# A gated recurrence with a soft mixture of experts on one core: TensorE fillers until a later plan time, the logarithm pinned ahead of the first tanh, new instruction lists

## The chip, the cores and the metric

The kernel runs on one core of one Trainium2 chip. The metric is the time of one execution on the device in microseconds (us); lower is better. The core has five instruction streams: PE (TensorE, matrix products and transposes), DVE (VectorE), ACT (ScalarE), POOL (GpSimd), and SP, which here only starts transfers (DMA). Each stream runs its instructions in the order in which the program lists them and waits on semaphores for the others.

## The reference

There are 4 sequences of 5056 tokens with 256 channels, so 20224 rows. A gated linear recurrence runs along each sequence, and its result goes through a soft mixture of 8 experts with 4 slots each (32 slots).

```python
# recurrence
sig_r, sig_i = sigmoid(r_gate), sigmoid(i_gate)
a_t  = exp(8 * sig_r * log(clip(sigmoid(a_param))))
norm = sqrt(max(1 - a_t * a_t, 1e-6))
h    = a_t[:, t] * h + (norm * sig_i * x)[:, t]        # over t, y[:, t] = h
# soft mixture of experts on x = y
logits = x @ phi
d = exp(logits - max over tokens) / sum over tokens
slot_out[e] = relu((d.T @ x)[e] @ w1[e]) @ w2[e]
c = exp(logits - max over slots) / sum over slots
out = c @ slot_out
```

The softmax over all tokens means that no output row can be made before the whole recurrence is done. The kernel has therefore a first part (the recurrence and running sums, to about 210 us), a short middle (the expert products, to about 232 us) and an output part.

## The kernel before, in words

Tokens are cut into 40 quads of 512 tokens (the last is shorter), and these into 21 units: quad 0 alone, then pairs, then quad 39 alone. In names, a number after a unit's letters is the unit (for U, YC and TY the quad), and .0 or .1 is the half of the channels. For one unit the steps are:

- Dr, Di, Dx (SP): loads of r_gate, i_gate and x, up to 1 MiB each.
- SR, SI (ACT, `mk_sr`, `mk_si`): tanh of the two gates. EX (ACT): a_t by exp, over two units at a time. RT (ACT): the square root. Exp and tanh share one table of ACT's functions, the square root needs another, and so does the logarithm, so ACT loads a table at each change. SA and LN (ACT, `e_sa`, `e_ln`) make the vector `ca` from a_param once: exp and then Ln, after which the table with exp and tanh is loaded. CA (DVE) clips it.
- SQ (POOL, DVE or ACT): a_t squared, a product of two SBUF tiles. U (POOL or DVE): the input gate times x, also two SBUF tiles. The string `IV` says for each quad how: D is one DVE instruction ((i+1)*x), E is i*x by one product, after which PE adds x while it transposes, P is an extra POOL step P1 (i+1) and then the product.
- TU (PE): transposes of the product into PSUM. ST (DVE): times the norm. SC (DVE): the recurrence as a scan, which needs the scan of the unit before. LG, TY (PE), YC (DVE or ACT), LE, AE (DVE), ES, DM (ACT), LD, PD (POOL): logits, y with tokens in partitions, running maxima, exponentials and sums over groups of four quads.

The middle is MT to SL (merging the sums), L1 and L2 (PE, the experts, with weights w1 and w2 loaded by SP), SO, RS and SW. The output part has, for each group, CT (PE), CM, CS (DVE), CE (ACT), RR, RB, RC, CN (POOL), TB (PE) and HE: the softmax over slots, transposed back. Then for each unit come OT (PE, 8 products into four banks of PSUM), OE (DVE or ACT, a copy of one bank) and OD (SP, the store).

Which engine does what in which order is written out: `ORDER` holds a list for each engine, and a list B for the order in which SBUF slots and POOL's and DVE's turns are claimed. The class `Planner` replays these lists with a duration for every step (its `alt` gives that on the other engine). The replay decides two more things: which buffer each step gets, and where PE gets a filler. A filler (`WU`, line 1220) is two transposes of the identity into a free bank. It is put wherever the replay finds PE with nothing to do before the plan time `WARMT`, and it stands in PE's list from then on. The replay ends when its last real step ends.

Of the kernel before, what the change touches and what calls it, by code (L numbers as in the profile page):

```python
# [26 lines left out]
IV = 'DDDEEEEEEEEEEEEEEDEEEEEEEDDPEPEPEPPPPPPD'  # L27
# [16 lines left out]
WARMT = 245.0  # L44
# [57 lines left out]
    ),  # L102
    "ACT": (
# [11 lines left out]
    ),  # L115
# [38 lines left out]
    ),  # L154
}
SWITCH = 0.09
# [1459 lines left out]
```

## Time and profile before

| | |
|---|---|
| runs | 290.07, 290.78, 291.12 us; median 290.78 |
| the profiled execution | 290.38 us, its span 288.4 us |
| busy share of the span | PE 86%, DVE 82%, ACT 83%, POOL 61% |
| transferred | 100.04 MB, HBM read 78.94 MB, written 20.71 MB |
| granted TensorE clock, mean | 0.943 of full speed |

The span runs from the first to the last instruction that the profiler shows; the execution's own time is 2.0 us longer. In the rows below a time is counted from the start of the span, "x8" is a count of instructions, and "<-" in square brackets names what ended the idle time ahead of an instruction. PEclk is the granted clock: 1.00 is 2.4 GHz and 0.50 is 1.2 GHz.

### The profile page before, as it was taken

Reading aid. Unit: us, or ns where it says so; the run is one execution under the profiler, and the core shown is the slowest. Engines: PE = TensorE matmul, PEld = TensorE weight load, DVE = VectorE, ACT = ScalarE, POOL = GpSimd, SP = SyncE. Lnnn points to the kernel's source line nnn. Section 1 sums busy time; section 2 is a strip of 40 time slices with the busy share of each in tenths; the row PEclk is TensorE's granted clock in tenths of the full one; section 3 lists DMA queues with packets and bytes.
Section 4 is the critical chain, followed back from the end, with each engine's and each line's share of the span. In section 5 each row is a group of like instructions: output and inputs, shape, how many; then the busy total and the mean of one; then the engine's idle time right before and its main releaser. Section 6 shows DMA issues by size and latency. Waiting matters only on the chain.

```text
span 288.4 us, 6115 instructions
## 1 busy us (share of the span) xinstructions
PE 247.2 (86%) x2523; PEld 190.0 (66%) x2523; DVE 235.9 (82%) x268; ACT 238.3 (83%) x231; POOL 175.2 (61%) x138
## 2 busy tenths in 40 slices
PE   8999798779887877988799989999899999968750
PEld 8999797549665645757468767666565576745540
DVE  0217999999999999999999999999979376885630
ACT  6999899999999989999999999999932267754450
POOL 4022969988999699996989989994030620031000
PEclk9999999979999999999999999999999999975755
DMA  7999999999994998959999999998930049999987
GB/s 279 431 420 424 417 418 418 423 419 423 410 408 157 384 405 331 401 169 353 370 350 400 330 427 414 379 393 352 347 136 2 5 164 414 416 415 409 399 335 330
DMA packets 14987, 100.04 MB, mean 347 GB/s; under 512 B 1904, under 2 KB 2160, under 8 KB 3184
## 3 DMA queue, kind: packets, MB, share of 16 engines
q1 hardware_dynamic: 14816, 99.65, 85.9%
q8 instruction: 20, 0.33, 0.4%
q14 instruction: 7, 0.06, 0.1%
q10 hardware_dynamic: 144, 0.00, 0.0%
HBM read 78.94 MB, written 20.71 MB: 346 GB/s over the span
## 4 chain that ended last, share of the span: by engine, by line
DVE 50%; PE 25%; ACT 10%; issue 10%; DMA 1%; POOL 0%; ACTq 0%; POOLq 0%; SPq 0%; DVEq 0%
DVE all_s L935 21%; DVE pair L915 13%; PE bank L1516 7%; DVE yn L974 5%; DVE all_s L848 3%; PE bank L1334 3%; PE one L1516 2%; ACT all_s L792 2%; PE bank L1380 2%; ACT all_s L863 2%; PE pair L892 2%; DVE all_s L1034 2%; PE bank L1490 2%; DVE all_s L827 2%; ACT yn L972 1%
## 5 line engine op out<-in xcount | busy, mean ns | idle before, releaser
L935 DVE TENSOR_TENSOR_SCAN all_s<-all_s,pair 128x1024 f32<-128x1024 f32 (+8 forms) x48 | 92.8, 1950 | 0.6
L829 POOL TENSOR_TENSOR all_s<-all_s 128x1024 f32<-128x1024 f32 x33 | 79.0, 2413 | 5.2 <-ACT all_s L807 4.8
L848 POOL TENSOR_TENSOR all_s<-all_s 128x1024 f32<-128x1024 f32 (+1 forms) x33 | 62.4, 1908 | 28.5 <-ACT all_s L863 26.1
L892 PE MATMUL pair<-ident,all_s 128*128 128x128 f32 x488 | 60.9, 276 | 8.8 <-DVE all_s L935 6.8
L892 PEld LDWEIGHTS pair<-ident,all_s 128*128 128x128 f32 x488 | 53.1, 140 | 18.2 <-DVE all_s L935 7.8
L958 PE MATMUL pair<-ident,all_s 128*128 128x128 f32 x316 | 41.8, 277 | 8.2 <-DVE all_s L935 6.2
L958 PEld LDWEIGHTS pair<-ident,all_s 128*128 128x128 f32 x316 | 34.4, 140 | 17.9 <-DVE all_s L935 9.9
L915 DVE SCALAR_TENSOR_TENSOR pair<-all_s,pair 128x1024 f32<-128x1024 f32 (+1 forms) x38 | 44.6, 1184 | 0.0
L1220 PE MATMUL one<-ident 128*128 128x128 f32 x342 | 41.6, 282 | 1.4 <-POOL ident masks.py:199 1.4
L863 ACT ACTIVATE all_s<-all_s,ca 128x2048 f32<-128x2048 f32 (+3 forms) x24 | 42.3, 1791 | 0.0
L1467 POOL TENSOR_TENSOR all_s<-all_s,rs_all 128x512 f32<-128x512 f32 (+3 forms) x12 | 10.5, 895 | 50.8 <-DVE rs_all L1464 50.8
L1220 PEld LDWEIGHTS one<-ident 128*128 128x128 f32 x342 | 39.8, 146 | 2.0 <-POOL ident masks.py:199 1.4
L875 ACT ACTIVATE all_s<-all_s 128x2048 f32<-128x2048 f32 (+2 forms) x21 | 37.2, 1807 | 2.3 <-DVE all_s L848 1.4
L807 ACT ACTIVATE all_s<-all_s 128x2048 f32<-128x2048 f32 (+2 forms) x21 | 37.8, 1806 | 0.0
L792 ACT ACTIVATE all_s<-all_s 128x2048 f32<-128x2048 f32 (+2 forms) x21 | 37.5, 1804 | 0.0
L1018 PE MATMUL one<-all_s,phi_sb 128*32 128x256 f32 (+1 forms) x328 | 24.8, 402 | 3.3 <-DVE all_s L1447 1.4
L1531 ACT COPY all_s<-bank 128x512 f32<-128x512 f32 (+1 forms) x34 | 18.8, 584 | 9.2 <-PE bank L1516 5.6
L1533 DVE COPY all_s<-bank 128x512 f32<-128x512 f32 (+1 forms) x29 | 18.5, 655 | 9.0 <-PE one L1516 4.3
L972 ACT COPY yn<-pair 128x1024 f32<-128x1024 f32 (+1 forms) x25 | 24.5, 991 | 0.9 <-PE pair L958 0.9
L1093 PE MATMUL one<-yn,eS 128*32 128x257 f32 x296 | 21.5, 386 | 0.2 <-ACT eS L1074 0.2
L974 DVE COPY yn<-pair 128x1024 f32<-128x1024 f32 x15 | 18.1, 1209 | 0.0
L1516 PE MATMUL bank<-all_s,lD 32*128 32x256 f32 x112 | 17.3, 471 | 0.3 <-ACT lD L1499 0.3
(116 smaller groups left out, 310.8 us busy)
## 6 DMA issues: line engine op xcount, KB each, us to landing
all_s<-in_r_gate_dram SPq DMA_DIRECT2D x19, 1024.0 KB, 8.0
all_s<-in_i_gate_dram SPq DMA_DIRECT2D x19, 1024.0 KB, 10.6
all_s<-in_x_dram SPq DMA_DIRECT2D x19, 1024.0 KB, 9.3
out_dram<-all_s SPq DMA_DIRECT2D x19, 1024.0 KB, 6.9
all_s<-in_moe_w_dram SPq DMA_DIRECT2D x16, 1024.0 KB, 8.6
all_s<-in_r_gate_dram SPq DMA_DIRECT2D x3, 256.0 KB, 3.0
all_s<-in_i_gate_dram SPq DMA_DIRECT2D x1, 512.0 KB, 6.1
all_s<-in_x_dram SPq DMA_DIRECT2D x1, 512.0 KB, 14.1
```

The costliest lines, as they stand in the source:

```text
L792: nc.scalar.activation(v, v, AF.Tanh, scale=0.5)
L807: nc.scalar.activation(v, v, AF.Tanh, scale=0.5)
L829: eng.tensor_tensor(out=o, in0=a, in1=b, op=ALU.mult)
L848: eng.tensor_tensor(out=t(Nb[(p, h)])[:, :c], in0=v, in1=v, op=ALU.mult)
L863: nc.scalar.activation(v, v, AF.Exp, scale=ca[:, h : h + 1], bias=ca[:, h : h + 1])
L875: nc.scalar.activation(v, v, AF.Sqrt, bias=f, scale=-f)
L892: nc.tensor.matmul(t(up)[:, i, m * P : (m + 1) * P], raw(nm, q)[:, m * D + h * P : m * D + (h + 1) * P], ident, is_transpose=True, start=( ...
L915: nc.vector.scalar_tensor_tensor(v, w, 1e-3 if gate_of(quads(p)[0]) == "S" else 0.5e-3, u, op0=ALU.max, op1=ALU.mult)
L935: nc.vector.tensor_tensor_scan(dst, dst, flat()[:, s0:s1], init, op0=ALU.mult, op1=ALU.add)
L958: nc.tensor.transpose(out=flat()[:, b * D + h * P : b * D + (h + 1) * P], in_=t(A[p])[:, h, i * QT + (b0 + b) * P : i * QT + (b0 + b + 1) ...
L1220: nc.tensor.transpose(out=t(b)[:, 0, :P] if b.tag == "pair" else t(b)[:, :P], in_=ident, identity=ident)
L1516: nc.tensor.matmul(t(op)[:, k * D : (k + 1) * D], t(hT)[r, (k0 + k) * P : (k0 + k + 1) * P], t(soRb)[r, :D], start=True, stop=True)
```

## The change

Five things are edited. `WARMT` goes from 245 to 280. SR depends on LN, so the logarithm comes ahead of the first tanh. A constant `HELD` = 0.7 is added to the planned time of most U and SQ on DVE. `LAG1`, a delay of the first large load in the replay, goes from 2.3 to 0.8. And `IV` and all lists are new. Counted from the lists, DVE loses SQ1.0, SQ7.0, SQ7.1, U1, U17 and U39 and gets SQ2.0, SQ2.1 and U8; ACT gets SQ20.1 from POOL; POOL has one step P1 more. YC stays at 15 on DVE and 25 on ACT.

```diff
-IV = 'DDDEEEEEEEEEEEEEEDEEEEEEEDDPEPEPEPPPPPPD'
+IV = 'DEDEEEEEDEEEEEEEEEEEEEEEEDDEPPEPPEPPPPPP'
...
-WARMT = 245.0
+WARMT = 280.0
+HELD = 0.7
...
-        "SA SR0 LN EX0.0 EX0.1 SR3 SI0 EX3.1 EX3.0 SR2 SR1 SI1 EX1.1 SI2 EX1.0 RT0.0 RT1.0 RT3.0 RT2.0 SI3 SR5 SR4 SI4 "
+        "SA LN SR0 SI0 EX0.1 EX0.0 SR3 EX3.1 SR1 SR2 EX3.0 EX1.0 EX1.1 SI1 SI2 RT0.0 RT2.0 RT1.0 RT3.0 SI3 SR4 SR5 SI4 "
...
-        "Dr0 Dr3 Di0 Dr2 Dr1 Di1 Dx0 Di2 Dx1 Dr4 Dx2 Di3 Dr5 Dx3 Di4 Dx4 Dr6 Dr7 Di5 Dr9 Di6 Dx5 Dx8 Dx7 Dx6 Di8 Dr8 Di7 "
+        "Di0 Dr0 Dr3 Dr1 Dr2 Dx0 Di2 Di1 Di3 Dx1 Dr4 Dx2 Dr5 Dx3 Di4 Dx4 Dr7 Dr6 Di5 Dx5 Di6 Dr9 Di7 Dx6 Di8 Dr8 Dx7 Dx8 "
...
-LAG1 = 2.3
+LAG1 = 0.8
...
-        SR[p] = add("ACT", f"SR{p}", 0.12 + 0.835 * c / 1024 * H, deps=[ld[("r", p)]], prio=pos_u(p) - 2, emit=e_sr,
+        SR[p] = add("ACT", f"SR{p}", 0.12 + 0.835 * c / 1024 * H, deps=[ld[("r", p)], t_ln], prio=pos_u(p) - 2, emit=e_sr,
...
-                   uses=[st[("i", q)], st[("x", q)]], alt={"DVE": 0.06 + 0.27 * n}, lock=True)
+                   uses=[st[("i", q)], st[("x", q)]], alt={"DVE": 0.06 + 0.27 * n + (HELD if 4 < q < NQ - 3 else 0.0)}, lock=True)
...
-                             alt={"DVE": 0.05 + 1.09 * c / 1024, "ACT": 0.12 + 0.835 * c / 1024}, lock=True)
+                             alt={"DVE": 0.05 + 1.09 * c / 1024 + (HELD if p > 2 else 0.0), "ACT": 0.12 + 0.835 * c / 1024}, lock=True)
```

Three places of the lists matter below. The first is the start of ACT's program, before: line 1121 is SA, 1124 LN, 1126 the table load behind it, 792 SR, 807 SI and 863 EX.

```order
L1121 ACTIVATE ca<-ca 128x2
L792 ACT_TABLE_LOAD
L792 ACTIVATE all_s<-all_s 128x2x512
L1124 ACT_TABLE_LOAD
L1124 ACTIVATE ca<-ca 128x2
L1126 ACT_TABLE_LOAD
L863 ACTIVATE all_s<-all_s,ca 128x512 x2
```

The same place of the change; every line number is one higher.

```order
L1122 ACTIVATE ca<-ca 128x2
L1125 ACTIVATE ca<-ca 128x2
L1127 ACT_TABLE_LOAD
L793 ACTIVATE all_s<-all_s 128x2x512
L808 ACTIVATE all_s<-all_s 128x1024
L864 ACTIVATE all_s<-all_s,ca 128x512 x2
```

LN now follows SA directly and needs no table of its own, and SR0 needs none behind it: two table loads are gone. SI0 has come ahead of the first EX.

The second place is DVE behind the scans of unit 3, before: line 848 is SQ (here SQ7.0 and SQ7.1), 974 YC, 1034 LE, 915 ST and 935 SC.

```order
L935 SCALAR_TENSOR_TENSOR all_s<-all_s,pair_77 128x1024
L848 TENSOR_TENSOR all_s<-all_s 128x1024
L974 COPY yn_63<-pair_75 128x4x256
L974 COPY yn_64<-pair_77 128x4x256
L848 TENSOR_TENSOR all_s<-all_s 128x1024
L974 COPY yn_65<-pair_75 128x4x256
L1034 TENSOR_SCALAR all_s,M<-one_71 128x384
L1034 TENSOR_SCALAR all_s,M<-one_70,M 128x512
L915 SCALAR_TENSOR_TENSOR pair_76<-all_s,pair_76 128x1024
```

The same place of the change, from ST3.0 to ST4.1; line 828 is U8.

```order
L975 COPY yn_63<-pair_75 128x4x256
L828 SCALAR_TENSOR_TENSOR all_s<-all_s 128x1024
L936 SCALAR_TENSOR_TENSOR all_s<-all_s,pair_76 128x1024
L916 SCALAR_TENSOR_TENSOR pair_75<-all_s,pair_75 128x1024
L936 SCALAR_TENSOR_TENSOR all_s<-all_s,pair_75 128x1024
L975 COPY yn_65<-pair_76 128x4x256
L975 COPY yn_64<-pair_77 128x4x256
L916 SCALAR_TENSOR_TENSOR pair_75<-all_s,pair_75 128x1024
L916 SCALAR_TENSOR_TENSOR pair_76<-all_s,pair_76 128x1024
```

The two squares have left DVE, one product U8 has come, and the two LE stand behind the ST of unit 4 now.

The third place is the end of PE's program: line 1516 is OT. Before, the last unit's products are the last rows.

```order
L1516 MATMUL bank_2104<-all_s,lD_67 128x256
L1516 MATMUL bank_2102<-all_s,lD_67 128x256
L1516 MATMUL one_70<-all_s,lD_67 128x256
L1516 MATMUL bank_2103<-all_s,lD_67 128x256
L1516 MATMUL bank_2104<-all_s,lD_67 128x256
L1611 UNCONDITIONAL_BRANCH
```

In the change the last products are followed by fillers (line 1221), of which the first eight stand here.

```order
L1517 MATMUL one_70<-all_s,eS_69 128x256
L1517 MATMUL bank_2067<-all_s,eS_69 128x256
L1221 MATMUL bank_2068<-ident 128x128 x2
L1221 MATMUL bank_2069<-ident 128x128 x2
L1221 MATMUL bank_2067<-ident 128x128 x2
L1221 MATMUL bank_2068<-ident 128x128 x2
L1221 MATMUL one_70<-ident 128x128 x2
L1221 MATMUL bank_2069<-ident 128x128 x2
L1221 MATMUL bank_2067<-ident 128x128 x2
L1221 MATMUL bank_2068<-ident 128x128 x2
```

There are 57 such fillers behind the last product, and 46 more between the first and the last OT, where the program before has 14, all in its first half.

## Rows read from the trace of the kernel before

**Rows 1.** Busy time by stretch: us, then PE, PEld, DVE, ACT, POOL, PEclk, DMA, GB/s.

```profile
40.00:60.00 20.00, 15.51 (x150) 13.22 (x149) 19.86 (x13) 19.97 (x12) 18.10 (x9) 1.00 1.01 420
...
80.00:100.00 20.00, 16.70 (x161) 13.14 (x160) 19.93 (x14) 19.43 (x13) 18.05 (x10) 1.00 0.77 307
...
180.00:200.00 20.00, 18.29 (x200) 12.83 (x202) 19.96 (x17) 19.86 (x23) 16.73 (x14) 1.00 0.95 371
...
240.00:260.00 20.00, 17.68 (x183) 12.61 (x176) 15.53 (x32) 13.58 (x28) 2.24 (x3) 0.88 1.01 416
260.00:280.00 20.00, 15.24 (x112) 10.80 (x110) 10.39 (x22) 10.50 (x23) 1.34 (x2) 0.59 0.92 377
```

**Rows 2.** ACT in order of time, start of the program: start, us, engine, line, operation.

```profile
4.29 1.28 ACT L792 ACT_TABLE_LOAD   x1 [0.47 <-DMA all_s<-in_r_gate_dram]
5.58 1.06 ACT L792 ACTIVATE all_s<-all_s 128x1024 f32<-128x1024 f32 x1
6.66 1.28 ACT L1124 ACT_TABLE_LOAD   x1
7.95 0.20 ACT L1124 ACTIVATE ca<-ca 128x2 f32<-128x2 f32 x1
8.18 1.28 ACT L1126 ACT_TABLE_LOAD   x1
...
27.21 1.28 ACT L875 ACT_TABLE_LOAD   x1
28.51 1.06 ACT L875 ACTIVATE all_s<-all_s 128x1024 f32<-128x1024 f32 x1
30.93 1.91 ACT L875 ACTIVATE all_s<-all_s 128x2048 f32<-128x2048 f32 x1 [1.37 <-DVE all_s L848]
```

**Rows 3.** DVE in order of time, 27 to 210 us.

```profile
27.98 2.92 DVE L848 TENSOR_TENSOR all_s<-all_s 128x1024 f32<-128x1024 f32 x1
30.82 1.28 DVE L915 SCALAR_TENSOR_TENSOR pair<-all_s,pair 128x512 f32<-128x512 f32 x2
...
56.55 1.82 DVE L848 TENSOR_TENSOR all_s<-all_s 128x1024 f32<-128x1024 f32 x1
...
60.56 2.77 DVE L848 TENSOR_TENSOR all_s<-all_s 128x1024 f32<-128x1024 f32 x1
...
97.07 2.06 DVE L827 SCALAR_TENSOR_TENSOR all_s<-all_s 128x1024 f32<-128x1024 f32 x1
...
189.09 1.20 DVE L915 SCALAR_TENSOR_TENSOR pair<-all_s,pair 128x1024 f32<-128x1024 f32 x1
...
205.01 0.69 DVE L827 SCALAR_TENSOR_TENSOR all_s<-all_s 128x512 f32<-128x512 f32 x1
```

**Rows 4.** ACT in order of time, the square roots of units 18 and 19.

```profile
187.10 1.91 ACT L875 ACTIVATE all_s<-all_s 128x2048 f32<-128x2048 f32 x1
```

**Rows 5.** POOL's products, kept apart by shape: count, busy us, mean ns, idle before.

```profile
L829 POOL TENSOR_TENSOR all_s<-all_s 128x1024 f32<-128x1024 f32 x33 | 79.0, 2413 | 5.2 <-ACT all_s L807 4.8
L848 POOL TENSOR_TENSOR all_s<-all_s 128x1024 f32<-128x1024 f32 x32 | 61.8, 1949 | 25.2 <-ACT all_s L863 22.8 <-DVE all_s L827 2.4
```

**Rows 6.** The output part in stretches of 2 us, columns as in the first group.

```profile
252.00:254.00 2.00, 0.44 (x2) 0.20 (x2) 1.75 (x7) 0.95 (x3) 1.04 (x1) 1.00 0.97 406
...
270.00:272.00 2.00, 1.13 (x12) 0.69 (x12) 1.58 (x4) 1.61 (x5) 0.00 (x0) 1.00 0.84 344
...
274.00:276.00 2.00, 2.00 (x23) 1.92 (x20) 0.42 (x1) 1.22 (x3) 0.00 (x0) 0.50 0.41 164
```

**Rows 7.** SP and PE in order of time: the stores, and PE's last product.

```profile
234.23 47.06 SPq L1540 DMA_DIRECT2D out_dram<-all_s  x21
277.46 0.63 PE L1516 MATMUL one<-all_s,lD 32*128 32x256 f32 x1
```

**Rows 8.** PE's fillers at the start: in order of time, then by stretch.

```profile
1.36 19.09 PE L1220 MATMUL one<-ident 128*128 128x128 f32 x152 [1.36 <-POOL ident masks.py:199]
15.00:20.00 5.00, 5.00 (x48) 5.00 (x47) 1.23 (x1) 5.00 (x4) 1.89 (x1) 1.00 1.01 419
```

106 rows, old and new, of the table ORDER are left out of this document.

## The prediction

> **What bounds the kernel now.** I read the busy time by stretches first [rows 1]. From 40 to 200 us DVE is busy 19.86 to 19.96 of every 20 us, ACT 19.43 to 19.97, and POOL 16.73 to 18.10. So two engines are full at once, and a third nearly. Transfers are saturated at the beginning (share 1.01, 420 GB/s at 40 to 60 us), but not later (0.77 at 80 to 100 us): there loads wait for free SBUF slots, not the engines for loads. Whatever shortens the first part must therefore shorten DVE and ACT both; the smaller gain counts.
>
> Next I read both engines in order of time. ACT loads three tables within 5 us [rows 2]: at 4.29 for the first tanh, at 6.66 for Ln, at 8.18 back to exp and tanh, 1.28 us each, and it works without a gap from there to 28.51, where the first root begins. Then it waits 1.37 us for a square on DVE (line 848). DVE's rows [rows 3] show that square at 27.98, taking 2.92 us; two products like it at 56.55 and 60.56 take 1.82 and 2.77, and a U at 97.07 takes 2.06. The same work on the same 128x1024 shape differs by over a microsecond, so some of these durations are waits inside the instruction: the shortest shows what the work costs, and what is above it appears where POOL runs a product at the same time. Much of DVE's "busy" is such a wait. Near the end of the first part, the root of unit 18 runs from 187.10 to 189.01 [rows 4] and DVE takes up that unit at 189.09 [rows 3]: DVE has no lead left to give there, so DVE gets through this place earlier only if ACT does.
>
> The output part is another regime. SP issues the first store at 234.23 [rows 7]; from then to the end of the span are 54.2 us, for 20.7 MB. Transfers run at 416 GB/s from 240 to 260 us [rows 1], and at that rate the stores need 49.8 us. So the output is bound by transfers, with some 2 us of hunger: the rows that show it are 274 to 276 us at 164 GB/s and 270 to 272 at 344 [rows 6]. Against 416 these lack 1.2 and 0.35 us. PE's granted clock is 0.50 (1.2 GHz) at 274 to 276 and 0.59 on average from 260 to 280; it fell after a stretch in which PE was busy 0.44 of 2 us (252 to 254).
>
> **The change, part by part.** *The logarithm.* Two of three table loads go, 2 x 1.28 = 2.56 us [rows 2], and the tanh of unit 0 needs r_gate only. But Di0 now stands ahead of Dr0, half a MiB, 1.25 us at 420 GB/s. The old tanh began at 5.58, after data at 4.29 and its table; the new one begins when its data come, 4.29 + 1.25 = 5.5. So that shift eats nothing, and ACT has 2.56 us of lead after it; with Ln's own 0.20 out of the way it is 2.7. Bounds: 0.6 us less if the first transfers are slower than 420, none of it if another load is late.
>
> *Squares and products off DVE.* Before its first ST at 30.82 [rows 3] DVE had the 2.92 us square. In the new list SQ1.0 and U1 are POOL's, while SQ2.0 and SQ2.1 come to DVE, in a stretch where it idles anyway. What gates the first ST now is root 0, at 28.51 + 1.06 - 2.7 = 26.9, and U2. U2's x comes 1 MiB later in the new list of loads, some 2.5 us, at about 25 us by 420 GB/s, so U2 ends at 26.5. DVE's chain thus starts near 27.2, 3.6 us earlier. Later on SQ7.0, SQ7.1, U17 and U39 leave it: the steps from each row's start to the next instruction are 1.74, 2.70, 1.99 and 0.8, together 7.2. U8 comes in, 1.1 us if POOL is idle and up to 2.4 more if it has just begun a product [rows 5]; I take 1.6, near the shortest row. DVE by itself gains 3.6 + 7.2 - 1.6 = 9.2 us.
>
> *ACT.* It gains the 2.7 us, and the 1.37 us wait for the square, which is done earlier now. SQ20.1 costs it 0.4, and one exp of the output (CE5) moves behind the end of this part. Of its other idle time (0.03, 0.57 and 0.14 in the stretches of [rows 1]) I grant it 1 us over the whole. That makes 5.0. Since DVE meets ACT at 189.09 without slack, the lead there is 5.0, not 9.2. Behind it DVE saves U39 alone: 0.7. So the first store comes **5.7 us earlier**, at 228.5; lower bound 2 (the tables alone, less the 0.6), upper bound 9.2 (DVE's).
>
> *POOL* takes on four squares and products more than it gives away and one step P1 (1.1 us): by 1.95 and 2.41 us apiece [rows 5] some 6 us, in idle time that three rows [rows 1] put at 2 us in 20. That is free as long as it is the slack between lists that fills.
>
> *Fillers in the output.* 46 lie between the products; each costs two transposes. At the start 48 transposes fill 5 us at full clock [rows 8], 0.104 each, 0.21 a filler: 10 us in all, in a part where PE idles and would otherwise go to 1.2 GHz. Held at 2.4 GHz, PE feeds the stores in time: I take back 1.2 of the 1.55 us of hunger. Bounds: 0 (the hunger is the evictions') to 2.
>
> *Fillers behind the last product.* Nothing waits for these 57, but the kernel ends only after them: 57 x 0.21 = 11.9 us at full clock. PE's last product ended at 278.1 [rows 7]; 5.7 earlier, and some 3 earlier again at full clock (half of the products after 255 ran at 1.2), it ends at 269.4, and the fillers at 281.3. The stores end at 288.4 - 5.7 - 1.2 = 281.5. The two meet: cost nothing in the likeliest case, up to 3 us if PE is not faster.
>
> **Two rules of the Trainium skill.** The trace has 1.31 us from the end of the first tanh to Ln, table load included [rows 2]. The Trainium skill (ScalarE: Activation LUTs, What ACT_TABLE_LOAD costs) gives a switch about 2.66 us, a load of 1.28 and a drain of about the same. By that the two loads would be worth 5.3 us and the sum 2.7 us less; the row decides against it. The second rule is a rival, and stands there.
>
> **The sum.** 288.4 - 5.7 - 1.2 = 281.5 us of span, plus 2.0 around it = 283.5; the median of the runs is 0.4 above the profiled execution, so **283.9 us**.
>
> **Rivals.** *The lead is eaten (2 in 10).* The new lists leave POOL and the loads no slack. U9, U17 and U18 come late on POOL behind SQ7.0 and SQ7.1, and DVE waits at ST5 or ST9 instead; or a load stalls for a slot where it did before (0.77 at 80 to 100 us). For it speaks POOL's 18 of 20 us [rows 1]; against it, that its idle time is still twice the 6 us. If 4 of the 5.7 us go: 288 us.
>
> *Fillers do not hold the clock (1 in 10, the other side).* The place is PE's end: at 1.2 GHz the 57 fillers take 23.8 us, and the last product stays at 278.1 - 5.7 = 272.4, so PE ends at 296.2 and the execution at 298. It decides from the point where the fillers take more than about 16 us, that is, if over a third of them run at half clock. Against it: from 15 to 20 us PE ran nothing but such fillers, and the granted clock was 1.00, 48 in 5 us [rows 8].
> The Trainium skill (TensorE: Matmul & The Clock Gate, Part 4: PE-mode transpose) says that transposes don't count as PE activity the way matmuls do, so the full clock doesn't engage for them, which would make this rival true. The trace disagrees for a stretch of 15 us without a matmul; after a long stretch at 1.2 GHz no row here shows it.
>
> *The output is not gated by PE and the first part moves by the tables alone (1 in 10).* 2.6 us: 288.2.
>
> *More than forecast (1 in 10).* The roots of the later units come earlier, as ACT's copies of y wait less; DVE's 9.2 us count: 280.
>
> **How the numbers follow.** The forecast has 5 in 10, the cases above 2, 1, 1 and 1. The measurement tells 0.5% (1.5 us) from no change, so faster is below 289.3. The forecast, the case with more, and the tables alone are faster; of the eaten lead I put a third at no change and a little at slower. That is 0.79 faster, 0.10 the same, 0.11 slower. The range from 280 (DVE's bound) to 289 (lead eaten) leaves out 2 in 10, mostly on the slow side.
>
> **What would show it.** The first ACT rows: one table load between Ln and tanh, the first root at about 26 us. DVE's first ST at 27 to 28, and no line 849 behind it. DVE and the root of unit 18 some 5 us earlier. The first store near 228.5. A granted clock of 1.00 to the end of the products, and transfers above 400 GB/s in every stretch of the output. PE's last filler near the last store's landing. Wrong it would be if DVE shows idle time or long waits between 60 and 190 us, or if PE outlasts the stores.

## The result, and the profile after

The changed kernel takes **286.62 us** (median of 4 runs, 286.23 to 286.97) against 290.70 for the kernel before, measured beside it: a ratio of 0.9861, 95% interval 0.9837 to 0.9886, so 1.4% faster. The forecast was 283.9 with a range of 280 to 289. The direction came out, and for the first part of the kernel the mechanism too; every stretch of the kernel gained less than forecast (table below).

The profiled execution took 286.92 us, its span is 284.9; before, these were 290.38 and 288.4. ACT's rows of the changed kernel in order of time (start, us, engine, line, operation, in brackets the idle time before it and what ended it) answer to [rows 2] and [rows 4]:

```profile
4.72 0.20 ACT L1122 ACTIVATE ca<-ca 128x2 f32<-128x2 f32 x1 [2.71 <-DMA ca<-in_a_param_dram]
4.96 0.20 ACT L1125 ACTIVATE ca<-ca 128x2 f32<-128x2 f32 x1
5.18 1.28 ACT L1127 ACT_TABLE_LOAD   x1
6.47 1.06 ACT L793 ACTIVATE all_s<-all_s 128x1024 f32<-128x1024 f32 x1
...
26.60 6.47 ACT L876 ACTIVATE all_s<-all_s 128x1024 f32<-128x1024 f32 x4
...
95.69 3.76 ACT L876 ACTIVATE all_s<-all_s 128x2048 f32<-128x2048 f32 x2 [0.45 <-POOL all_s L849]
114.76 1.91 ACT L808 ACTIVATE all_s<-all_s 128x2048 f32<-128x2048 f32 x1 [1.23 <-DMA all_s<-in_i_gate_dram]
...
183.57 1.91 ACT L876 ACTIVATE all_s<-all_s 128x2048 f32<-128x2048 f32 x1
```

One table load stands between Ln and the first tanh, as foretold. But the first tanh begins at 6.47 and not at 5.5, because the parameter row landed late. The four roots from 26.60 on run without the old wait of 1.37. The root of unit 18 is 3.5 us earlier than in [rows 4]. On the way ACT waits twice, 0.45 and 1.23; the kernel before had two other waits there, 0.54 for PE and 0.82 for POOL.

DVE's and POOL's rows, the first to be held against [rows 3]:

```profile
27.69 0.70 DVE L916 SCALAR_TENSOR_TENSOR pair<-all_s,pair 128x512 f32<-128x512 f32 x1 [0.47 <-ACT all_s L876]
...
60.10 1.23 DVE L916 SCALAR_TENSOR_TENSOR pair<-all_s,pair 128x1024 f32<-128x1024 f32 x1 [1.30 <-ACT all_s L876]
63.17 1.23 DVE L916 SCALAR_TENSOR_TENSOR pair<-all_s,pair 128x1024 f32<-128x1024 f32 x1 [1.83 <-PE pair L893]
...
185.52 1.23 DVE L916 SCALAR_TENSOR_TENSOR pair<-all_s,pair 128x1024 f32<-128x1024 f32 x1 [0.40 <-ACT all_s L876]
```

```profile
65.94 2.36 POOL L830 TENSOR_TENSOR all_s<-all_s 128x1024 f32<-128x1024 f32 x1
70.11 0.70 POOL L1051 TENSOR_SCALAR lD<-all_s,M 128x512 f32<-128x512 f32 x1 [1.81 <-DVE all_s L1035]
```

DVE now waits, for ACT, for PE, and at unit 18 for ACT again. And POOL waits 1.81 us at 68.3 for a reduction on DVE. Busy time by stretch (columns as in [rows 1]) shows what that means:

```profile
54.00:56.00 2.00, 0.20 (x2) 0.00 (x0) 1.97 (x2) 2.00 (x2) 1.96 (x2) 0.98 1.03 430
56.00:58.00 2.00, 1.29 (x6) 1.32 (x7) 2.00 (x3) 1.98 (x2) 2.00 (x2) 0.50 1.00 418
...
60.00:80.00 20.00, 17.70 (x170) 14.77 (x163) 17.96 (x16) 19.97 (x14) 18.18 (x11) 0.93 1.02 421
80.00:100.00 20.00, 17.34 (x174) 12.51 (x173) 19.96 (x17) 19.50 (x14) 20.00 (x12) 1.00 0.89 355
100.00:120.00 20.00, 16.79 (x169) 12.86 (x169) 19.89 (x17) 18.76 (x14) 20.00 (x11) 1.00 1.00 412
...
274.00:276.00 2.00, 2.00 (x20) 2.00 (x19) 0.00 (x0) 0.00 (x0) 0.00 (x0) 1.00 1.03 430
```

The granted clock is 0.50 (1.2 GHz) from 56 to 62 us, after a stretch in which PE was busy 0.20 of 2 us. POOL, which had 18.05 of 20 us before [rows 1], has no idle time left from 80 to 120. In the output the clock stays at 1.00 (2.4 GHz) with PE running only fillers, and the 164 GB/s of [rows 6] at 274 to 276 us have become 430.

The stores, and the output's last group of products (count, min/median/max ns, first and last start), answering to [rows 7]:

```profile
231.22 7.68 SPq L1541 DMA_DIRECT2D out_dram<-all_s  x5
```

```profile
L1517 PE MATMUL bank<-all_s,eS x112: 374/374/478, 231.3 to 268.5; 32*128 32x256 f32 x112
```

The last product ends 37.6 us behind the first store (268.8), where it was 43.9 before (278.1). The 3.5 us by which the span is shorter divide thus:

| stretch | before | after | gain | forecast |
|---|---|---|---|---|
| start to first root | 28.51 | 26.60 | 1.9 | 2.7 |
| first root to DVE's row of unit 18 | 160.58 | 158.92 | 1.7 | 2.3 |
| that row to first store | 45.14 | 45.70 | -0.6 | 0.7 |
| first store to end of span | 54.2 | 53.7 | 0.5 | 1.2 |

(The forecast of 2.3 is the 1.37 and the 1 us granted to ACT, less about 0.1.)

### The profile page after: what moved, and what is told of

Its sections match the earlier page's. It is cut to its first block, busy times and chain, and to the rows that moved or that the text cites. A ratio compares the mean times of both kernels' runs of the same rounds, so it can differ in the third digit from the quotient of the medians.

```text
span 284.9 us, 6358 instructions
## 1 busy us (share of the span) xinstructions
PE 256.6 (90%) x2655; PEld 198.9 (70%) x2655; DVE 229.9 (81%) x262; ACT 236.2 (83%) x233; POOL 181.5 (64%) x141
## 4 chain that ended last, share of the span: by engine, by line
ACT 31%; PE 29%; DVE 26%; issue 9%; DMA 4%; DVEq 0%; ACTq 0%; SPq 0%
DVE all_s L936 13%; DVE pair L916 7%; PE bank L1517 6%; ACT all_s L864 6%; PE bank L1221 6%; ACT all_s L793 5%; ACT all_s L876 5%; ACT yn L973 4%; ACT all_s L808 4%; DVE yn L975 3%; DMA all_s<-in_i_gate_dram 3%; PE pair L893 3%; PE bank L1335 3%; PE one L1381 2%; PE one L1221 2%
## 5 line engine op out<-in xcount | busy, mean ns | idle before, releaser
L830 POOL TENSOR_TENSOR all_s<-all_s 128x1024 f32<-128x1024 f32 (+1 forms) x35 | 82.8, 2381 | 6.4 <-DMA all_s<-in_x_dram 3.3
L849 POOL TENSOR_TENSOR all_s<-all_s 128x1024 f32<-128x1024 f32 x33 | 64.1, 1963 | 16.3 <-ACT all_s L864 14.4
L893 PE MATMUL pair<-ident,all_s 128*128 128x128 f32 x496 | 63.8, 282 | 10.2 <-DVE all_s L936 4.8
L893 PEld LDWEIGHTS pair<-ident,all_s 128*128 128x128 f32 x496 | 56.2, 144 | 19.3 <-issue 6.6
L959 PE MATMUL pair<-ident,all_s 128*128 128x128 f32 x316 | 42.5, 278 | 5.9 <-DVE all_s L936 3.1
L959 PEld LDWEIGHTS pair<-ident,all_s 128*128 128x128 f32 x316 | 34.1, 140 | 17.1 <-DVE all_s L936 7.1
L1221 PE MATMUL one<-ident 128*128 128x128 f32 x338 | 43.0, 280 | 2.1 <-POOL ident masks.py:199 1.4
L1532 ACT COPY all_s<-bank 128x512 f32<-128x512 f32 (+1 forms) x39 | 20.4, 575 | 7.5 <-PE bank L1517 4.6
L1019 PE MATMUL one<-all_s,phi_sb 128*32 128x256 f32 (+1 forms) x328 | 23.1, 383 | 1.0 <-DVE all_s L936 0.6
L1534 DVE COPY all_s<-bank 128x512 f32<-128x512 f32 (+1 forms) x26 | 17.2, 676 | 7.9 <-PE bank L1517 6.2
L1221 PE MATMUL bank<-ident 128*128 128x128 f32 x150 | 21.7, 277 | 0.1
L1221 PEld LDWEIGHTS bank<-ident 128*128 128x128 f32 x150 | 16.8, 140 | 3.2 <-ACT all_s L1532 1.7
```

Source lines behind the costliest of these rows:

```text
L830: eng.tensor_tensor(out=o, in0=a, in1=b, op=ALU.mult)
L849: eng.tensor_tensor(out=t(Nb[(p, h)])[:, :c], in0=v, in1=v, op=ALU.mult)
L893: nc.tensor.matmul(t(up)[:, i, m * P : (m + 1) * P], raw(nm, q)[:, m * D + h * P : m * D + (h + 1) * P], ident, is_transpose=True, start=( ...
L959: nc.tensor.transpose(out=flat()[:, b * D + h * P : b * D + (h + 1) * P], in_=t(A[p])[:, h, i * QT + (b0 + b) * P : i * QT + (b0 + b + 1) ...
L1221: nc.tensor.transpose(out=t(b)[:, 0, :P] if b.tag == "pair" else t(b)[:, :P], in_=ident, identity=ident)
```

## The experiments

The places are those of the table above, in each kernel's own profiled execution; the time is the median of all its runs. Where an expectation counts from 25.30 us, it means the table load ahead of the first root at 26.60.

| kernel | first root | unit 18 | first store | to end | us | ratio to before, 95% |
|---|---|---|---|---|---|---|
| no pin | 30.23 | 191.33 | 237.02 | 53.7 | 291.79 | 1.0019 to 1.0062 |
| r_gate 0 first | 28.68 | 187.20 | 232.90 | 53.7 | 286.64 | 0.9853 to 0.9909 |
| before, pin alone | 27.60 | 188.21 | 233.36 | 53.7 | 289.38 | 0.9927 to 0.9981 |
| before, fillers alone | 28.61 | 189.86 | 235.00 | 53.8 | 290.22 | 0.9972 to 1.0006 |
| fillers to 245 | 26.59 | 184.84 | 230.53 | 53.4 | 285.31 | 0.9797 to 0.9848 |
| fillers to 268 | 26.59 | 183.97 | 229.66 | 53.6 | 285.85 | 0.9810 to 0.9872 |
| squares of unit 7 on DVE | 26.57 | 184.98 | 230.97 | 53.4 | 286.31 | 0.9843 to 0.9887 |
| copy of maxima on ACT | 26.52 | 184.61 | 230.29 | 53.7 | 286.35 | 0.9837 to 0.9888 |
| LD1 late | 26.91 | 184.56 | 230.26 | 54.0 | 286.22 | 0.9828 to 0.9867 |
| y of unit 3 three times | 26.59 | 185.58 | 231.28 | 53.7 | 286.00 | 0.9821 to 0.9860 |
| both, fillers to 245 | 26.58 | 183.53 | 229.22 | 53.1 | 285.27 | 0.9786 to 0.9839 |
| CT7 behind, fillers to 245 | 26.58 | 185.00 | 231.24 | 53.2 | 286.39 | 0.9838 to 0.9885 |

The places scatter from one execution to the next. The changed kernel, those with fillers to 245 and to 268, with the copy of maxima on ACT and with CT7 behind run the same instructions up to unit 18, and reach it at 185.52, 184.84, 183.97, 184.61 and 185.00: 1.55 us apart with nothing edited ahead of it. In the old lists the kernel before and the one with fillers alone reach it 0.77 us apart (189.09 and 189.86). A smaller shift of a place can't be put down to an edit by one profile.

**The pin undone in the changed kernel.**

```diff
-        "SA LN SR0 SI0 EX0.1 ...
+        "SA SR0 LN SI0 EX0.1 ...
-        SR[p] = add("ACT", ..., deps=[ld[("r", p)], t_ln], ...
+        SR[p] = add("ACT", ..., deps=[ld[("r", p)]], ...
```

> The changed kernel without the pin: the logarithm again behind the first tanh, so there are three table loads at the start. Theory (ACT sets the end): the first root begins some 1.6 to 2.6 us later than 25.30, and the first store and the end come as much later: 288.2 to 289.2 us. Rival (the lead from the tables is eaten by load or POOL waits before 190 us in the changed kernel, and the gain came from DVE's relief or from the output): under 0.5 us, 286.6 to 287.1.

It took 291.79 us, 5.2 more than the changed kernel, beyond the theory's 2.6. ACT in order of time:

```profile
5.87 1.28 ACT L793 ACT_TABLE_LOAD   x1 [0.99 <-DMA all_s<-in_r_gate_dram]
7.16 1.06 ACT L793 ACTIVATE all_s<-all_s 128x1024 f32<-128x1024 f32 x1
8.24 1.28 ACT L1125 ACT_TABLE_LOAD   x1
9.54 0.20 ACT L1125 ACTIVATE ca<-ca 128x2 f32<-128x2 f32 x1
9.76 1.28 ACT L1127 ACT_TABLE_LOAD   x1
```

The first tanh is 0.7 later than with the pin, because its table load now stands behind the data's arrival and not ahead of it; the two other loads with Ln take 2.8 more (8.24 to 11.05). So the first root comes 3.6 us later: with the new order of loads, the pin is worth 3.6 and not 2.7. Of the further 2.2 us up to unit 18 the trace shows where, not all of the why: PE's clock is 0.50 from 62 to 68 us, DVE then waits 0.80 and 2.30 us for PE, and ACT at 82 and 93 us for PE too, 0.71 and 1.03. The rival is refuted. Without the pin the new lists are even a little slower than the kernel before (1.0019 to 1.0062): they are made for an early ACT.

**The pin alone, in the kernel before** (the same two edits the other way round).

> The kernel before with one part of the change alone: the logarithm pinned ahead of the first tanh; lists and fillers as before. Theory (the term of the tables by itself): ACT's first root begins 2.6 us earlier than 28.51, or earlier by what remains before the square on DVE (25.9 to 28.5), ACT keeps a lead of 2.0 to 2.6 us up to the root of unit 18, and the end comes as much earlier: 288.1 to 288.7 us. Rival (the old lists wait elsewhere, first of all for the square of unit 0 on DVE, which with DVE's full row takes the lead away): under 0.5 us, 290.2 to 290.7.

289.38 us, 1.3 less than before, between theory and rival. ACT in order of time:

```profile
9.88 1.92 ACT L792 ACTIVATE all_s<-all_s 128x2048 f32<-128x2048 f32 x1 [1.58 <-DMA all_s<-in_r_gate_dram]
...
27.60 1.06 ACT L875 ACTIVATE all_s<-all_s 128x1024 f32<-128x1024 f32 x1
30.07 1.92 ACT L875 ACTIVATE all_s<-all_s 128x2048 f32<-128x2048 f32 x1 [1.40 <-DVE all_s L848]
```

DVE's square, the row that begins at 27.98 in [rows 3]:

```profile
27.11 2.92 DVE L848 TENSOR_TENSOR all_s<-all_s 128x1024 f32<-128x1024 f32 x1
```

In the old order of loads the time won is waited away: 1.58 us for the next r_gate, so the first root is only 0.9 earlier, and the wait for DVE's square stays at 1.40. That 0.9 then reaches the first store undiminished (234.23 against 233.36). This does not tell whether ACT or DVE carries it: DVE's square begins 0.87 earlier as well, and DVE is busy 99% of the time from there to 211 us in either kernel. The times show that the pin gains here (0.9927 to 0.9981), and that the whole change gains far more (4.1 us) than the pin alone (1.3 us) and the rest of it without the pin (a loss).

**The old order of the first two loads.**

```diff
-        "Di0 Dr0 Dr3 Dr1 ...
+        "Dr0 Di0 Dr3 Dr1 ...
```

> The changed kernel with the loads of r_gate 0 and i_gate 0 in their old order (r_gate 0 first). Theory: the first tanh began at 6.47 and not at the forecast 5.5 because i_gate 0 stands ahead on the queues and the parameter row landed 1.1 us later (4.7 against 3.6); here the row lands near 3.6 and the first tanh begins near 5.5; ACT has no gap up to the first root, so the root of unit 0 begins 0.8 to 1.0 us earlier than 25.30, and as the end follows ACT, the first store comes some 0.9 us earlier: 285.7 us. Rival A: the lead is eaten later by loads that wait for slots (the wait of the tanh at 114.76 for i_gate 16 grows from 1.23 to about 2.1): 286.6 us, no change. Rival B: i_gate's tanh, which comes next, now waits for its data instead: no change from the start on.

286.64 us: no change in the median, as rival B has it (single runs scatter more, 286.15 to 288.63, and the profiled one is the 288.63, so its places in the table, 2 us late from the first root on, are not those of a middling run). ACT in order of time:

```profile
3.60 0.20 ACT L1122 ACTIVATE ca<-ca 128x2 f32<-128x2 f32 x1 [1.58 <-DMA ca<-in_a_param_dram]
...
5.35 1.06 ACT L793 ACTIVATE all_s<-all_s 128x1024 f32<-128x1024 f32 x1
7.80 1.06 ACT L808 ACTIVATE all_s<-all_s 128x1024 f32<-128x1024 f32 x1 [1.40 <-DMA all_s<-in_i_gate_dram]
...
16.75 1.91 ACT L793 ACTIVATE all_s<-all_s 128x2048 f32<-128x2048 f32 x1 [1.50 <-DMA all_s<-in_r_gate_dram]
```

The parameter row does land 1.1 us earlier, so it is i_gate 0's load (512 KB at once; r_gate 0 goes in two of 256 KB) that delays it in the changed kernel, and the first tanh begins at 5.35. But 1.40 us are then waited for i_gate 0, and 1.50 for another r_gate. An early start is worth what the loads behind it can keep up with.

**Fillers: none in the output, or none behind the last product.**

```diff
-WARMT = 280.0
+WARMT = 245.0
```

In the other kernel the new value is 268.0.

> The changed kernel with fillers only up to the place where they ended before: none between the products of the output and none behind the last. Theory: the granted clock falls to 0.50 some time in the output again, products there come late, and stretches with stores under 350 GB/s return as in the kernel before; 0.5 to 1.5 us slower: 287.1 to 288.1. Rival A: the stores have enough in hand, no change: 286.6. Rival B: the fillers behind the last product cost something at the end (the stores trickle out over the last 2 us in the changed kernel), and without them it is 1 us faster: 285.6.

> The changed kernel with the fillers between the products of the output but few or none behind the last product. Theory (the trailing fillers end at 281.4 and the stores at 283.1, so they cost nothing): 286.6 us. Rival (they delay the last stores or the end of the kernel): 285.6 us.

285.31 and 285.85 us: not slower, so the theory of the first falls. In that kernel, the last group of products as above, and a stretch of the output:

```profile
L1517 PE MATMUL bank<-all_s,eS x104: 374/374/788, 230.6 to 266.8; 32*128 32x256 f32 x104
```

```profile
275.00:280.00 5.00, 0.00 (x0) 0.00 (x0) 0.00 (x0) 0.00 (x0) 0.00 (x0) 0.50 1.01 423
```

Some products run at half clock (788 ns for the longest, 478 with fillers), yet the last one ends 37.0 us behind the first store, and the stores are not hungry: 423 GB/s here, and no stretch of 2 us from 232 to 280 is under 389. The new order alone has put the products nearly 7 us further ahead (43.9 before). From first store to end it takes 53.4 without fillers, 53.6 with the inner ones, 53.7 with all. Over all profiled executions of the new lists it is 53.1 to 53.4 in the three kernels with fillers to 245 and 53.4 to 54.0 in the seven with all fillers. So the fillers buy nothing here; by the means of these (53.2 and 53.7) they rather cost about 0.5. The medians are 1.3 and 0.8 below the changed kernel's, which is more than this; in the profiles 0.7 and 1.6 us lie ahead of the first store, where the three programs do the same work. There the clock at 56 us differs between single executions (last section).

**Fillers alone, in the kernel before.**

```diff
-WARMT = 245.0
+WARMT = 280.0
```

> The kernel before with another part alone: fillers through the output, as in the change. Theory: the granted clock stays at 1.00 to the end of the products, the stretch at 274 to 276 us with 164 GB/s fills up, and the end comes 0.5 to 1.5 us earlier: 289.2 to 290.2 us. Rival: nothing, since the stores then trickle out at the end as in the changed kernel (290.7), or the fillers outlast the stores, as PE's last product is later here (1 to 3 us slower).

290.22 us, 0.9972 to 1.0006: no change that can be told. From first store to end it takes 53.8 against 54.2, with the last product 39.9 us behind the first store (43.9 before): there the products end 4 us earlier against the stores, and the stretch is 0.4 shorter. That these 0.4 are the fillers' is not shown: with the pin alone, where the output has the old lists and no fillers beyond those of the kernel before, it is 53.7 as well. There the clock falls too (0.50 from 254 to 260), but the last product ends 41.2 us behind the first store, and no stretch of 2 us from 236 to 280 is under 369 GB/s. So the hungry stretch of [rows 6] belongs to that execution, not to every one of the old output.

**The squares of unit 7 back on DVE.**

```diff
 "DVE":  ... ST3.0 SC3.0
-  YC3.0 YC2.0 ST4.0
+  SQ7.0 YC3.0 YC2.0 SQ7.1 ST4.0
 "POOL": ... SQ6.1
-  SQ7.0 SQ7.1 SQ6.0
+  SQ6.0
```

> The changed kernel with the two squares of unit 7 back on DVE (between the copies of y of units 3 and 2), off POOL. They cost DVE 3 to 4.5 us of busy time. Theory (the forecast's: DVE has slack against ACT, which is what counts): the 3 us that DVE waits at 58 to 63 us take most of it, and the end comes 0 to 1.5 us later: 286.6 to 288.1. Rival (DVE is a bound of its own there): 4 us later, 290.6. Third: POOL, full from 80 to 120 us, is what eats the lead; relieved by 4 us, it gives 1 us back: 285.6.

286.31 us, no change. DVE is busy 19.93 and 19.65 of 20 us from 40 to 80 in this kernel (18.73 and 17.96 in the changed one): its waits take the squares (1.69 and 1.21 us) in. So DVE's own time was not the bound, as the forecast had it. POOL, relieved, gives nothing back:

```profile
69.86 0.69 POOL L1051 TENSOR_SCALAR lD<-all_s,M 128x512 f32<-128x512 f32 x1 [2.17 <-DVE all_s L1035]
```

It waits for the same reduction until 69.86, in place of 70.11.

**The masking step LD1 later on POOL.**

```diff
-  SQ6.0 U10 U9 LD0 U11 LD1 U12 PD1
+  SQ6.0 U10 U9 LD0 U11 U12 LD1 PD1
```

> The changed kernel with one pair of steps swapped in POOL's list: the masking step LD1 behind the product U12, not ahead of it. In the changed kernel POOL waits 1.81 us for that step at 68.3 us (the row at 70.11, released by DVE's line 1035) and is then full to 120 us, and the tanh for i_gate 16 waits 1.23 us at 114.76. Theory: in this stretch POOL sets the pace, through the slots that its products free; POOL's wait goes, what follows on it runs 1.3 to 1.8 us earlier, the wait at 114.76 shrinks to under 0.3, and the first store comes 1.2 to 1.7 us earlier than 231.22, at 229.5 to 230.0: 285.0 to 285.5 us. Rival: PE, whose transposes of that step come later now, or ACT with the roots of the next units, sets it: no change, 286.6.

POOL's wait is gone (20.00 of 20 us from 60 on), the wait for i_gate 16 halves, and the first store comes at 230.26, 1.0 earlier, although the start was 0.3 later:

```profile
113.81 1.91 ACT L808 ACTIVATE all_s<-all_s 128x2048 f32<-128x2048 f32 x1 [0.58 <-DMA all_s<-in_i_gate_dram]
```

The median moved by 0.4 us only (286.22), within both intervals. And unit 18 at 184.56 lies within what the five executions without this edit show (183.97 to 185.52). In the one with fillers to 268, whose clock was back at 1.00 at 62 us, POOL took LD1 at 68.82 after a wait of 0.54, and ACT waited 0.34 us for i_gate 16. So the trace shows that POOL's wait goes with the edit; that the end comes earlier by it is not shown.

**PE kept busy at 54 us.** The transposes for the copy of y of unit 3 are written three times to the same place.

```diff
-                for b in range(nb):
+                for b in [*range(nb)] * (3 if q == 3 else 1):
```

> The changed kernel with the transposes of the copy of y of unit 3 (line 959, 53.11 us) written three times to the same place, 24 and not 8, which fills PE's wait of 2.50 us for the scan behind them; DVE takes up the result at 56.48 only. Theory: PE's granted clock falls to 0.50 at 55.95 because PE was busy 0.20 of 2 us before it; with the place filled it stays 1.00 to 63, the transposes at 56.71 take 0.27 and not 0.42 us each, DVE's waits of 1.30 and 1.83 us at 58 to 63 shrink together to under 1.5, DVE's reduction that POOL waits for at 68.3 comes 1.3 us earlier, and the first store 1.0 to 1.5 us earlier than 231.22: 285.2 to 285.7 us. Rival A: the clock falls all the same, there or some us later, since transposes alone do not hold it at this place: no change. Rival B: the clock holds but nothing behind DVE's waits moves: no change.

```profile
54.00:56.00 2.00, 1.94 (x18) 1.70 (x16) 1.96 (x2) 2.00 (x2) 1.95 (x2) 1.00 1.04 434
56.00:58.00 2.00, 1.30 (x12) 1.29 (x12) 2.00 (x3) 1.98 (x2) 2.00 (x2) 1.00 0.99 414
...
66.00:68.00 2.00, 2.00 (x11) 2.00 (x10) 2.00 (x3) 1.99 (x2) 2.00 (x1) 0.50 0.98 410
```

The clock holds at 56 us, and falls at 65 instead (rival A's "some us later"). DVE then waits 1.00 for PE at 69 us, and the first store is where it was, 231.28. Median 286.00. POOL's step LD1 and ACT's tanh for i_gate 16:

```profile
68.25 0.69 POOL L1051 TENSOR_SCALAR lD<-all_s,M 128x512 f32<-128x512 f32 x1
```

```profile
114.86 1.92 ACT L808 ACTIVATE all_s<-all_s 128x2048 f32<-128x2048 f32 x1 [1.94 <-DMA all_s<-in_i_gate_dram]
```

So POOL takes LD1 1.9 us earlier and without a wait, as the theory has it, and still i_gate 16 lands no earlier, although SP issues its load at 105.53 and not at 106.38. LD1 is therefore not all that holds this load; what else does is open.

**Both edits, with fillers to 245.**

> Both of the edits at 53 to 70 us (LD1 behind U12, the transposes of the copy of y of unit 3 three times), and fillers only up to where they ended in the kernel before. Theory: the two edits remove the same lateness of 1.3 to 1.8 us, so they do not add; without the fillers in the output the time from the first store to the end is 53.4, as it was without them: first store at 229.5, 284.5 to 285.0 us. Rival: they add, first store at 228.5: 283.8 us.

Here the profiled execution shows the clock at 1.00 from the start to 245 us, ACT without a wait over 0.35 us from 5 to 205, and the stores begin at

```profile
229.22 11.75 SPq L1541 DMA_DIRECT2D out_dram<-all_s  x7
```

2.0 us earlier than in the changed kernel, between the theory's 229.5 and the rival's 228.5. But unit 18, at 183.53, is only 0.4 us ahead of the earliest of the five executions without these edits (183.97). The median is 285.27 (284.26 to 285.71), the lowest of all, 1.9% under the kernel before (0.9786 to 0.9839). Its interval overlaps those of the kernels with fewer fillers, and the kernel with fillers to 245 alone has 285.31. So neither the times nor, beyond 0.4 us, the profile speak for the two edits. The clock between 56 and 70 us goes with the place of unit 18 only in part: 183.53 here without a fall, 183.97 with the shortest fall of the five (fillers to 268), 185.52 with 0.50 throughout 56 to 62 (the changed kernel), but 185.58 with as short a fall at 65 instead. What sets the rest is open.

**The 0.6 us lost between unit 18 and the first store.** DVE's copy of the row of maxima takes 1.35 us in the changed kernel, beside a memset on POOL; it was put on ACT. And CT7 was put behind AC10 and MC again.

```diff
-        a = add("DVE", "MR", 0.21, ... nc.vector.tensor_copy(
+        a = add("ACT", "MR", 0.21, ... nc.scalar.copy(
```

> The changed kernel with the little copy of the row of maxima (line 1272) on ACT and not on DVE. Theory: in the changed kernel it took 1.35 us, and 0.22 before, because POOL's memset of 128x2048 runs beside it and the DVE copy waits inside the instruction; on ACT it takes under 0.5 us, what follows it between the last scan and the first store begins 1.0 us earlier, and the first store too: 285.6 us. Rival (the products on PE ahead of its user set that place, so nothing behind it moves): 286.6 us, no change.

```diff
-  MT TE11 CT7 AC10.0 AC10.1 MC AC11.0 CT4
+  MT TE11 AC10.0 AC10.1 MC CT7 AC11.0 CT4
```

> The changed kernel with fillers only up to where they ended before (run already: 285.31 us), and with PE's transposes of weights CT7 behind the products AC10 and MC and not ahead of them, as it was before the change. From DVE's row for unit 18 to the first store the changed kernel takes 45.70 us and the kernel before 45.14. Theory: CT7 ahead of AC10 is what costs here, 0.66 us of PE on the chain from the last scan to the first store; with it behind, the stretch is 45.1, and the time 284.7 us. Rival: the chain goes by DVE's accumulation and the row of maxima, no change: 285.3 us; or CT7 is then late for the first layer, 0.5 us slower.

The copy is not the cause; for CT7 the run does not tell. With the copy on ACT the stretch is 45.68, as before the edit (45.70), and DVE waits for PE's product instead:

```profile
208.38 0.48 DVE L1109 SCALAR_TENSOR_TENSOR accS<-accS,dm,bank 128x257 f32<-128x257 f32 x1 [1.61 <-PE bank L1094]
```

With CT7 behind, the stretch is 46.24, and the time 1.1 over the kernel with fillers to 245. It is no clean test, though: the planner put fillers into the free place, and AC10 did not start earlier against the last scan. What the traces show is that the transposes TE10 on PE come 2.40 us behind the start of the last scan before and 3.38 after, with PE busy with copies of y, logits and sums in between. The last scan on DVE and TE10 on PE, before:

```profile
207.79 0.75 DVE L935 TENSOR_TENSOR_SCAN all_s<-all_s,pair 128x256 f32<-128x256 f32 x1
```

```profile
210.19 0.41 PE L1065 MATMUL bank<-ident,lD 128*128 128x128 f32 x2 [0.24 <-ACT yn L972]
```

And after:

```profile
203.43 0.74 DVE L936 TENSOR_TENSOR_SCAN all_s<-all_s,pair 128x256 f32<-128x256 f32 x1
```

```profile
206.81 0.44 PE L1066 MATMUL one<-ident,lD 128*128 128x128 f32 x2 [0.21 <-DVE lD L1055]
```

AC10 then starts at 208.08, where its input from ACT was ready at 207.66, so CT7 can hold it by 0.4 us at most. That the order of PE's steps costs the 1.0 us was not tried.

## Why the prediction came out as it did

*In the first part the mechanism was right.* ACT sets the time to unit 18. DVE waits there for ACT (0.40 at 185.52), and takes 2.9 us of extra work without a change. The 9.2 us of DVE did not count; "more than forecast" is refuted. By its own sign ("long waits between 60 and 190 us" on DVE) the prediction would be wrong: DVE waits 1.30 and 1.83 at 60. But a DVE relieved by 9.2 us behind an ACT relieved by 5.0 had to wait, so the sign did not fit the sum. That the time fell within the range owes something to the range's width: of the 6.9 us forecast for the span, 3.5 came.

*"That shift eats nothing"* is the step that failed in the term of the logarithm. I let the first tanh begin at 5.5, when its data come. It needs Ln now, Ln needs the parameter row, and that landed at 4.7 and not at 3.6, behind the other first load: 6.47. Its own data were late as well, since r_gate 0 ends a wait only at 5.87 in the kernel without the pin. The term measured 1.9 where I had 2.7. The 1.37 us came as forecast. The pin's worth hangs on the order of loads: 0.9 in the old one, 3.6 in the new.
The Trainium skill (ScalarE: Activation LUTs, What ACT_TABLE_LOAD costs) gives 2.66 us for a switch; the changed kernel again has 1.31 from the end of Ln to the tanh (5.16 to 6.47), and the measurement decides.

*The 1 us granted to ACT* became 0.3, and the rival "the lead is eaten" came true in part: not at U9, U17 or U18, but at the masking step LD1, late on POOL behind a late DVE behind a PE at 1.2 GHz, and at a load that comes late. How much of it goes that way is open: five executions of the same instructions take 157.38 to 158.92 us for this stretch, and the changed kernel's profile is the longest, so its 0.3 is also the luck of the execution. I had put POOL's added 6 us into its idle time, which it had on average; from 70 to 120 us it has none. With both edits the stretch takes 156.95 us, 2.0 less than in that profile and 0.4 less than the shortest of the five.

*U39's 0.7* is there: the last scan is 4.4 earlier (207.79 to 203.43), where DVE's row of unit 18 was 3.6. But the first store is only 3.0 earlier: 1.35 us are lost behind the last scan, 1.0 of it by TE10 in PE's list. I had not read that list at all, as if nothing else changed there.

*Fillers in the output, 1.2 us.* This step failed: 0.5 measured, and not by the fillers. In the new lists they gain nothing, and in the old output 53.7 us occur without them. The new lists put the products nearly 7 us further ahead of the stores, so a slow PE starves none. The hunger in [rows 6] is gone with or without fillers, and with it gone the output still takes 53.4 to 53.7 us: it was worth 0.5 to 0.8 us, where I took back 1.2, and its cure was not the clock.

*Fillers behind the last product* end before the kernel does, as forecast: PE ends at 281.4, the span at 284.9. "Cost nothing" holds to about 0.5 us only, by which the kernels with all fillers take longer from the first store on. The rival that they don't hold the clock is refuted: PE ran nothing but transposes from 270 us on, and the granted clock was 1.00, at 20 in 2 us.
By the Trainium skill (TensorE: Matmul & The Clock Gate, Part 4: PE-mode transpose) transposes do not bring the full clock; the trace disagrees, here and from 54 to 58 us with the transposes written three times (1.00).

## What to carry to other kernels

An engine with little idle time on average, POOL here, has none in the stretch where it matters: look where the new list leaves it full, since a step that waits there (LD1) can hand its lateness on to what follows. Removing work ahead of the first step only pays as far as the loads keep up, so time the pin and the order of loads together. Before paying for a faster clock, see whether the work it speeds up can simply be done earlier. And before a shift of 1 us in one profile is put down to an edit, see how far executions of the same instructions lie apart.

## What the runs showed of the hardware

The same place of the same program does not get the same clock each time: it was 0.50 in all of 56 to 62 us in the changed kernel, and with fillers to 268 it was 0.90 from 56 to 58, 0.50 to 60, 0.75 to 62 and then 1.00, with the first store 1.6 us earlier; PE had been busy 0.19 to 0.20 of the 2 us before in both. The row with fillers to 268:

```profile
56.00:58.00 2.00, 1.31 (x10) 1.34 (x11) 2.00 (x3) 1.98 (x2) 2.00 (x2) 0.90 0.99 414
```

A parameter row of 1 KB, issued on ACT's queue, was there for ACT at 4.65 to 5.04 us in the ten kernels in which SP's first load was one of 512 KB, and at 3.60 to 3.94 in the four in which it was one of 256 KB.

A DVE copy of 1x128 took 0.22 us in the kernel before, beside an idle POOL, and 1.35 in the changed one. POOL and DVE in order of time there:

```profile
207.18 1.81 POOL L1317 MEMSET all_s<- 128x2048 f32 x1
```

```profile
207.71 1.35 DVE L1272 COPY mrep<-mmax 1x128 f32<-1x128 f32 x1
```

The copy ends at 209.06, 0.07 us behind the end of the memset (208.99). The Trainium skill (SBUF — State Buffer, Who interferes with whom) says that a DVE copy can contend with GpSimd for a shared port pair, and that whoever issues first has it for the whole instruction while the other is blocked; the trace agrees.
